# The seventh key chunk of an attention head as one full-width matmul, late queries and keys loaded in whole rows, and a new written order of the work

## The chip, the cores and the metric

The kernel runs on one core of one Trainium2 chip. The metric is the device time of one execution in microseconds (us). An effect of about 1% (4 us of 401) is what a measurement of this kernel can tell from no change.

## The reference

Attention with a squared ReLU in place of the softmax, for 8 batches of 12 heads, 448 positions and 64 values per head, and behind it a gated feed-forward block on the 3584 tokens:

```python
# q, k, v: (8, 12, 448, 64)
scores = scale * np.matmul(q, k.transpose(0, 1, 3, 2))     # scale = 1/8
attn = np.maximum(scores, 0.0) ** 2 / S                     # S = 448
attn_out = np.matmul(attn, v)
x = attn_out.transpose(0, 2, 1, 3).reshape(B * S, H * D)    # (3584, 768)
g, val = x @ w_gate, x @ w_val                              # (768, 1536) each
out = (gelu(g) * val) @ w_out                               # (1536, 768)
```

Inputs and the output are float32; the kernel computes in bfloat16 with float32 sums.

## The kernel before, in words

**The array in quarters.** Heads are 64 wide, so every matmul of the steady work uses one 64x64 quarter of TensorE: two row groups (where the operands' partitions lie) by two column groups (where the output's partitions lie). Four quarters work side by side. A helper `mm` (L365 in the profile) records all of these matmuls, so they share one line and are told apart by their tiles.

**Attention.** The 448 positions of a head are cut into 7 key chunks of 64. Two chunks `w` and `w + 4` (`w` = 0, 1, 2) make one score unit of two heads: four matmuls of 448 columns, one in each quarter, into two banks of PSUM (tile `sp`). ScalarE applies the ReLU to the whole unit (tile `rl`, L714), VectorE squares (tile `attnT`, L728), mostly two units at once. The chunk with index 3 (`VC - 1`) has no partner. Before, its units take four heads at once, and the queries are halved: each head's matmul of 64 keys and 448 queries is run as two of 224 queries, one in each column group, so that a unit has eight matmuls of 224 columns. A head pair's values (`add_values`) are sums over the chunks: row group 0 takes chunks 0, 1, 2, row group 1 takes chunks 4, 5, 6, and chunk 3 is split between the two row groups, each with 224 columns. The result is copied as `xT` (L792).

**Feed-forward.** Some blocks of 128 features are computed plainly: gate (`xT,wg`) and value (`xT,wv`) matmuls of 448 columns in `add_gate_value`. For the others (`NPB`: 0, 1, 2, 3, 4, 4, 6, 6 units for batches 0 to 7) seven products of half size take the place of eight (`add_pair`, 224 columns each); these need sums of weight blocks (`add_pair_sums`, VectorE, L870, tiles `ws`) and of token blocks (`ts`). The output product works in the same manner on two chunks of tokens (`add_product`, 384 columns, tiles `s`, `wt`, `osb`), 14 groups lettered a to n.

**Loads.** All loads of inputs go through the POOL queue, in one written order: queries, keys and values of batches 0 and 1 with the weights between them, then the "late" batches 2 to 7. Batches 0 and 1 get their transposed queries and keys from TensorE (`add_transposes`, L646, four heads at a time for batch 1); the late ones from VectorE's copy `qkr` (L475) and two DMA transposes on the SP queue. Before, late queries and keys come in two pieces per tensor: the first four chunks of four heads, then the last three.

**What sets the order.** The table `START` orders batch 0's attention. `LINE` lists the feed-forward units (a digit: a plain gate or value unit of that batch; `3A4`: a seven-product unit; `f2`: an output product). Scores and values of batches 1 to 7 are placed between them by a formula (`starts`, `LEAD`, `SHIFT`). `run_plan`, a planner with costs in us, walks this list: among the next 40 units (`AHEAD`) it takes the first whose inputs it expects to be there, and it also decides where the row-group-1 half of each unit, the copies, the stores and the DMA transposes go. So the list is a preference, and the program's order is the planner's. Banks of PSUM: four for the feed-forward and two pairs for scores; once the scores of batch 1 are done (`WIDE`) one pair is handed to the feed-forward.

Of the kernel before, what the change touches and what calls it, by code (L numbers as in the profile page):

```python
# [11 lines left out]
LINE = """  # L12
0 0 0 0 0 0 0 0 0 0 0 0 0 0 0 0 0 0 0 0 0 0 0 0 1 1A1 1 2 1A6 2 2 1 1A7 1A2 1A5 2 a1 2 a2 2A1 1A4 1
1 1 1A3 1 2 1 2A2 a6 1 2A7 a7 2 1 a5 1 1 2A6 2 2 1 1 1 1 a3 1 1 a4 1 1 b1 b7 c1 b2 b6 2A4 2 c6 b4 b5
c7 c5 2B1 2B6 c4 2B2 c3 b3 2A5 2 c2 2B7 2B4 2B5 2A3 2 3A1 2 3A2 2 2B3 2 2 3A6 3A7 d7 d1 3B1 d2 4C1
3B2 3 3C1 3B7 3 d6 3 e1 d4 3C7 3 3C6 3 3B6 e7 3B4 e6 3A4 3A5 3 3 3 3C2 3 3B5 3 3 d5 3C4 3A3 3C5 d3
4A1 4C2 3B3 3C3 e5 3 4A7 f1 f2 f6 e4 f7 4C7 4 e2 4C6 4A2 e3 g7 4B1 f5 4B6 4 4A6 4B2 g1 4B7 4 g2 4A5
4C5 4A4 4B4 4B5 f4 4D7 4D1 4C4 4 5B1 5 4D6 4D5 4A3 4 g6 4 g5 4C3 4B3 f3 4 5 5B2 4D2 4D4 g3 4D3 5C1
g4 5B6 5B7 5C2 5B5 5A1 4 5A6 5 5C7 5A7 5A2 5 5B4 5D1 h1 5A4 5D6 5D2 h6 5C6 h7 5 5D7 5D5 5A5 6A1 5B3
5 5C5 5C4 5A3 5C3 5D4 6B1 5 5D3 5 6A2 6B2 h4 i1 i2 6B7 6A6 i7 h5 6A7 h2 6D1 6F7 6D7 h3 j1 6D6 6C1  # L20
6D2 i6 j7 6E1 j6 6C7 6C2 6E7 i5 i4 6C6 6B6 6A5 6A4 6E6 6A3 6F1 6B4 6B5 6C5 6D5 6D4 6F6 i3 6B3 6F5
6C4 j5 6D3 6E2 6F2 6E5 6F4 6C3 6F3 6E4 6E3 7E7 j2 7E1 7B1 k1 k7 7E2 7A1 7B2 7B7 k2 7B6 7E6 j4 7C1 k6
7A2 l7 7C7 7C6 7A7 7B4 7C2 l1 7B5 7B3 k5 7A6 7F1 j3 7D1 7E5 7F7 7F2 7A5 k4 7F6 7E4 l6 7D7 7C4 7D2
7F4 7D6 7D5 7D4 7D3 l2 7F5 7A4 7C5 7C3 7E3 7A3 l5 l4 7F3 m1 n1 m7 k3 l3 m2 m6 n6 m5 n7 n4 m3 n5 n2
m4 n3
# [7 lines left out]


SHIFT = "-183 -79.5 40.75 1.75 -343.75 -112 43.75 -179.5 27.25 -513.5 -447.25 0.25"
# [60 lines left out]
class Unit:  # L96


    def __init__(self, at, los, his, box=None, closer=None, prev=None):
        self.at, self.los, self.his, self.box, self.closer, self.prev = at, los, his, box, closer, prev  # L100
        self.begun = False
        self.short = False
# [3 lines left out]
BANK = 0.3  # L106


def run_plan(queues, pools, units, banks, arrivals, together, fill, blocks, span):
# [48 lines left out]
    def next_unit(short):  # L158
        best = None
        now = max(free["PE0"], floor)  # L160
        for u in units[:AHEAD]:
# [16 lines left out]
            if u.box is not None:  # L178
                k, end = None, None
                for n, c in banks.items():  # L180
                    x = 0.0 if c is None else c.end
                    if x is not None and (end is None or x < end):
                        k, end = n, x
                if k is None:
                    continue
                t = max(t, end + BANK)
            if short and t > now:
                continue
            t = max(t, now)
            if best is None or t < best[0]:  # L190
                best = (t, u, k)
                if t <= now:
                    break
# [5 lines left out]
    while left:  # L199
# [33 lines left out]
        if isinstance(op, tuple):  # L233
            _, u, k = op
            u.begun = True
            units.remove(u)
            if k is not None:
                u.box["k"] = k
                banks[k] = u.closer()
            queues["PE0"][at["PE0"]:at["PE0"]] = u.los  # L240
# [36 lines left out]
def kernel(  # L277
# [42 lines left out]
    SINGLE = "3"  # L320
    RING_M, RING_G = 5, 4
# [17 lines left out]
    loaded = tc.tile_pool(name="lpool", bufs=2), tc.tile_pool(name="hpool", bufs=RING_H)  # L339
# [75 lines left out]
    def load_qk(b, i, h0, h1, deps=()):  # L415

        src = (q, k)[i]
        m, r0 = divmod(h0, 4)

        def emit(c0, c1):  # L420
            if (b, m) not in qk16:
                qk16[b, m] = hpool.tile([128, 4, SC * D], bf16, name="qk16", tag="qk16")
            cols = slice(c0 * D, c1 * D)
            return nc.gpsimd.dma_start(  # L424
                qk16[b, m][HALF[i], r0:r0 + h1 - h0, cols],
                src[b, h0:h1].rearrange("h (p c) d -> p h (c d)", c=SC)[:, :, cols])
# [39 lines left out]
    def add_dma_transposes(b, m, deps=()):  # L466
# [23 lines left out]
        copy = Op("DVE", 0.62, emit_copy, [wait, *(regrouped[n - 2] if n > 1 else ())], lag=0.15, prio=1)  # L490
# [43 lines left out]
    def next_scores(at):  # L534

        n = len(units)
        if at > WIDE and n % SB == 0 or wide:
# [48 lines left out]
    def then(at, step, los, his, box=None, closer=None):  # L586

        if not isinstance(at, list) and at > FIXED:
# [3 lines left out]
            later.append(Unit(at, los, his, box, closer))  # L592
# [84 lines left out]
    def add_scores(at, b, u):  # L677
# [9 lines left out]
        def emit(j, pr):  # L687
# [73 lines left out]
    def add_values(at, b, pr):  # L761
        box = {}

        order = ([0, 3, 1, 2] if pr % 2 else [0, 1, 2, 3], [3, 0, 1, 2])
# [3 lines left out]
        def emit(i, w):  # L768
            if 0 not in box:
                box[0] = new_bank(box["k"], x_op[b, pr])  # L770
            if (i, w) == (1, VC - 1) or last and (i, w) == (0, 1):
                wait_lower(box)
            for j in range(2):
                o = box[0][HALF[j], 0:S]
                a = att[b, pr, w][HALF[i], j, :]
                if w < VC - 1:
                    ins = mm(o, v16[b, pr // 2][HALF[i], 2 * (pr % 2) + j, w + i, :], a, i, j,
                       i == 0 and w == 0, i == 1 - last and w == VC - 2)
                else:
                    ins = mm(o.rearrange("d (c p) -> d c p", c=SC)[:, :, i * P // 2:(i + 1) * P // 2],  # L780
                       v16[b, pr // 2][HALF[i], 2 * (pr % 2) + j, (1 - i) * (VC - 1), :],
                       a[:, (pr % 2) * S // 2:(pr % 2 + 1) * S // 2].rearrange(
                           "k (c p) -> k c p", c=SC), i, j, False, False)
# [11 lines left out]
        ops = [[Op(f"PE{i}", 0.189 if w < VC - 1 else 0.095, lambda i=i, w=w: emit(i, w),  # L795
# [18 lines left out]
        if last:  # L814
            ops[1][0].after = ops[0][1]
            for o, p in zip(ops[1], ops[1][1:]):
                p.after = o
            ops[0][2].deps.append(ops[1][3])
            for i in range(2):
                lower.append((at - 0.6, ops[0][i]))  # L820
                lower.append((at, ops[0][i + 2]))
            for hi in ops[1]:
                pairs.append(("with", ops[0][1], hi))
# [285 lines left out]
    def add_sums(gr):  # L1109
# [20 lines left out]
        def add(n, x, y, op, into=None, after=(), cuts=(0, KH)):  # L1130
# [14 lines left out]
            for f0, f1 in zip(cuts, cuts[1:]):  # L1145
# [8 lines left out]
                for b in {b for t, _ in tiles for b, _ in chunks[t]}:  # L1154
                    if st["made_by"](b, 0) is u_op[b, 0]:
# [4 lines left out]
    def add_product(at, gr, name, final):  # L1160
# [100 lines left out]
        for b in {b for tile in chunks for b, _ in tile}:  # L1261
            if st["made_by"](b, 0) is u_op[b, 0]:
                reads_u.setdefault(b, []).append(ops[1][-1])
        then(at, RS, *ops, box if name in opens else None, lambda: st["read", stages_last[stage]])
# [38 lines left out]

    work = []
    flow = [[("g", b, fc, g) for fc in range(2 * NPB[b], FC) for g in range(2)] for b in range(B)]
    line = []
    for x in LINE.split():
        if len(x) == 1:
            line.append(flow[int(x)].pop(0))
        elif len(x) == 3:  # L1310
            line.append(("7", int(x[0]), "ABCDEFGHIJKL".index(x[1]), x[2]))
        else:
            line.append(("p", "abcdefghijklmn".index(x[0]), x[1]))
    assert not any(flow)
# [182 lines left out]
```

## Time and profile before

| | |
|---|---|
| median of 3 runs | 401.29 us (399.08 to 402.02) |
| span of the profiled execution | 394.9 us; the page gives this execution by its span alone, and the median lies 6.39 us above it |
| instructions in the span | 22904, of them 10570 matmuls and 10573 weight loads |
| TensorE busy | 386.3 us, 98% |
| VectorE, ScalarE busy | 309.6 us (78%), 258.7 us (66%) |
| granted TensorE clock | 0.998 |
| read and written in HBM | 48.76 MB, 11.01 MB |

The span is the time from the first to the last instruction that the profiler recorded. Busy time of TensorE is that of modelled, overlapping matmuls: it says that the engine was not empty, not how full it was. A row of a group gives the count, the busy time, the mean duration of one in ns, and the idle time of its engine just ahead of it with what ended it. POOL's rows are the issue of loads; when the data lands is seen from who waits for it.

### The profile page before, as it was taken

To read this page: it belongs to the slowest core of one execution; us is meant where nothing else is said; L and a number is where in the kernel's file an instruction comes from. 1 tells how busy PE (TensorE), PEld (TensorE's weight loads), DVE (VectorE), ACT (ScalarE), POOL (GpSimd) and SP (SyncE) were. 2 spreads that over 40 slices of the span, in tenths; PEclk is the share of its full clock that TensorE was granted. 3 is DMA by queue.
4 is the path that set the end of the run, shared out by engine and by line. 5 is a ranking of instruction groups with operands and counts; after the bars stand their busy time and mean duration, and the time that the engine had idled before them with its cause. 6 is when DMAs were issued, how large, how long until landed. Compare 5 with 4: busy or idle time off the path is not lost.

```text
span 394.9 us, 22904 instructions
## 1 busy us (share of the span) xinstructions
PE 386.3 (98%) x10570; PEld 358.4 (91%) x10573; DVE 309.6 (78%) x522; ACT 258.7 (66%) x401; POOL 97.2 (25%) x156
## 2 busy tenths in 40 slices
PE   7999999999999999999999999999999999999995
PEld 3458889999999999999999999989999999999994
DVE  3885779968797499999797779758988999866772
ACT  5866872357677767787786478765787886535541
POOL 7656523322233323232332123310211000000000
PEclk9999999999999999999999999999999999999999
DMA  8999999988999969887999598880763501121134
GB/s 110 186 199 199 197 209 185 112 103 83 161 148 175 152 85 143 93 132 121 113 148 108 124 122 111 139 83 11 103 105 56 125 6 43 45 45 45 43 85 120
DMA packets 85567, 45.12 MB, mean 114 GB/s; under 512 B 46048, under 2 KB 82400, under 8 KB 85472
## 3 DMA queue, kind: packets, MB, share of 16 engines
q0 software_dynamic: 46944, 24.39, 49.9%
q1 hardware_dynamic: 37888, 18.49, 26.4%
q8 instruction: 82, 1.34, 1.4%
q10 hardware_dynamic: 640, 0.79, 0.6%
q14 instruction: 13, 0.11, 0.1%
HBM read 48.76 MB, written 11.01 MB: 151 GB/s over the span
## 4 chain that ended last, share of the span: by engine, by line
PE 93%; DVE 2%; DMA 2%; POOL 1%; issue 1%; ACT 0%; ACTq 0%; POOLq 0%
PE ff L365 85%; PE sp L365 7%; DMA qk<-in_k_dram 2%; DVE attnT L728 1%; PE sp L646 1%; POOL qk L424 1%; DVE xT L792 0%; PE ff L646 0%; ACTq L1241 0%; ACT osb L1225 0%; ACT rl L714 0%; PE ff L567 0%; DVE osb L1223 0%; DVE qkT L650 0%; POOL ident masks.py:199 0%
## 5 line engine op out<-in xcount | busy, mean ns | idle before, releaser
L714 ACT ACTIVATE rl<-sp 128x896 bf16<-128x896 f32 x168 | 152.1, 919 | 50.4 <-PE sp L365 45.1
L365 PE MATMUL ff<-xT,wg 64*64 64x224 bf16 (+1 forms) x2304 | 183.7, 299 | 0.6 <-issue 0.6
L365 PEld LDWEIGHTS <-wv 64*64 64x64 bf16 x2304 | 127.7, 107 | 4.4
L365 PEld LDWEIGHTS <-wg 64*64 64x64 bf16 x2304 | 123.3, 107 | 5.0 <-issue 0.5
L365 PE MATMUL ff<-xT,wv 64*64 64x448 bf16 x1056 | 120.8, 349 | 0.0
L728 DVE TENSOR_TENSOR attnT<-rl 128x1792 bf16<-128x1792 bf16 (+1 forms) x98 | 92.2, 952 | 6.6 <-ACT rl L714 6.2
L365 PEld LDWEIGHTS <-ws 64*64 64x64 bf16 x1872 | 92.3, 107 | 1.4 <-issue 1.0
L365 PEld LDWEIGHTS <-s 64*64 64x64 bf16 x1344 | 81.6, 107 | 1.8
L365 PE MATMUL ff<-attnT,v 64*64 64x448 bf16 (+1 forms) x768 | 79.7, 326 | 0.7 <-DVE attnT L728 0.6
L365 PE MATMUL ff<-ts,wv 64*64 64x224 bf16 x1248 | 78.7, 256 | 0.0
L365 PE MATMUL ff<-ts,ws 64*64 64x224 bf16 x1248 | 77.6, 256 | 0.0
L365 PE MATMUL sp<-qkT 64*64 64x448 bf16 (+1 forms) x768 | 74.6, 328 | 0.7 <-issue 0.3
L365 PE MATMUL ff<-wo,s 64*64 64x384 bf16 x672 | 63.4, 323 | 0.0
L966 DVE TENSOR_TENSOR part<-ff,part 128x448 f32<-128x448 f32 x78 | 47.5, 622 | 20.1 <-PE ff L365 16.4
L365 PEld LDWEIGHTS <-uT 64*64 64x64 bf16 x1008 | 62.5, 107 | 0.7
L365 PE MATMUL ff<-wt,s 64*64 64x384 bf16 x672 | 61.4, 322 | 0.0
L365 PE MATMUL ff<-wo,uT 64*64 64x384 bf16 x672 | 60.7, 322 | 0.0
L962 ACT COPY part<-ff 128x448 f32<-128x448 f32 x78 | 41.3, 534 | 12.4 <-PE ff L365 11.2
L443 POOL DMA_DIRECT2D v<-in_v_dram x48 | 29.6, 620 | 80.3 <-ACT rl L714 44.3
L365 PEld LDWEIGHTS <-v 64*64 64x64 bf16 x768 | 44.7, 107 | 4.1 <-issue 1.7
L424 POOL DMA_DIRECT2D qk<-in_q_dram x43 | 27.6, 642 | 80.0 <-ACT rl L714 59.5
L1049 DVE TENSOR_TENSOR uT<-gel,ff 128x448 bf16<-128x448 bf16 x44 | 27.3, 620 | 22.4 <-PE ff L365 11.0
(51 smaller groups left out, 423.9 us busy)
## 6 DMA issues: line engine op xcount, KB each, us to landing
out_dram<-osb SPq DMA_DIRECT2D x48, 192.0 KB, 3.3
v<-in_v_dram POOLq DMA_DIRECT2D x48, 128.0 KB, 4.1
wg<-in_moe_w_gate_dram POOLq DMA_DIRECT2D x6, 384.0 KB, 10.4
wv<-in_moe_w_val_dram POOLq DMA_DIRECT2D x6, 384.0 KB, 11.0
wo<-in_moe_w_out_dram POOLq DMA_DIRECT2D x4, 576.0 KB, 14.9
qk<-in_q_dram POOLq DMA_DIRECT2D x18, 128.0 KB, 3.5
qk<-in_k_dram POOLq DMA_DIRECT2D x18, 128.0 KB, 4.3
qk<-in_q_dram POOLq DMA_DIRECT2D x18, 96.0 KB, 3.8
```

Of the source, the lines that this page charges most:

```text
L365: ins = nc.tensor.matmul(o, lhsT, rhs, start=start, stop=stop, skip_group_check=onto, tile_position=(P * row, P * col))
L424: return nc.gpsimd.dma_start(qk16[b, m][HALF[i], r0:r0 + h1 - h0, cols], src[b, h0:h1].rearrange("h (p c) d -> p h (c d)", c=SC)[:, :, cols])
L443: return nc.gpsimd.dma_start(v16[b, m][HALF[i], h0 % 4:h0 % 4 + h1 - h0, :, :], v[b, h0:h1].rearrange("h (p c) d -> p h c d", c=SC)[:, :, ...
L646: blocks.add(nc.tensor.transpose(t[HALF[j], c, :], src[:, 2 * r + j, c, :], ident[:, :], tile_position=(0, P * j)))
L714: relu.ins = nc.scalar.activation(duo["rl"][:, u % 2, :, :], box[0][:, :, 0:S], AF.Relu).ins
L728: nc.vector.tensor_tensor(a[:, part], duo["rl"][:, part], duo["rl"][:, part], op=ALU.mult)
L962: rd.ins = nc.scalar.copy(st["t", name][:, :], box[0][:, 0:S]).ins
L966: rd.ins = nc.vector.tensor_tensor(t[:, :], box[0][:, 0:S], t[:, :], op=ALU.add).ins
L1049: u_op[b, fc].ins = nc.vector.tensor_tensor(uT[b][:, fc, :], gel.pop((b, fc))[:, :], box[0][:, 0:S], op=ALU.mult).ins
```

## The change

1. **The seventh chunk whole.** In a score unit of chunk 3, each head now has one matmul of 448 queries; the two head pairs of the unit lie in the two column groups. So the unit has four matmuls of 448 columns in place of eight of 224. In `add_values` chunk 3 then belongs to one row group alone: to row group 0 for even head pairs (four steps there, three in row group 1), to row group 1 for odd ones (three and four). This is 96 matmuls fewer in the scores and 96 fewer in the values, each with its weight load: 384 instructions.
2. **Late queries and keys in whole rows.** A load takes two heads and all seven chunks (`64x2x448`) in place of four heads and four or three chunks.
3. **The order.** `LINE` now names every unit of batches 1 to 7: `s` a score unit, `v` a value unit, `t` a transpose unit of batch 1, `w0` to `w5` the weight sums of a block; the formula and `SHIFT` are gone. `START` and `run_plan`'s rules stay, but for an option (`more`, `full`, `COVER`) that no caller uses. `WIDE` now counts score units (44) and means the same place.

On TensorE, around the third group of transposes of batch 1 (`qk16`: heads 8 to 11), with the values of batch 1's first pair (`attnT,v16`) and gate and value units of batch 0 (`xT,wg`, `xT,wv`), before:

```order
L365 MATMUL ff_1020<-attnT_935,v16_534 64x448
...
L365 MATMUL ff_975<-xT_393,wg2_131 64x448
...
L365 MATMUL ff_1020<-attnT_935,v16_534 64x7x32
...
L365 MATMUL ff_1039<-xT_393,wv2_137 64x448
...
L646 LDWEIGHTS qk16_689
L646 MATMUL sp_1051<-ident_121,qk16_689 64x128
```

The same place of the change:

```order
L385 MATMUL ff_930<-attnT_837,v16_516 64x448
...
L385 MATMUL ff_890<-xT_385,wg1_130 64x448
...
L385 MATMUL ff_958<-xT_385,wv1_136 64x448
...
L665 LDWEIGHTS qk16_662
L665 MATMUL sp_971<-ident_121,qk16_662 64x128
```

The transposes, which stood behind the first units of weight block 2 (`wg2`, `wv2`), now stand ahead of them, among those of block 1. Ahead of them stood 398 matmuls of 448 columns and 58 of 224; now 382 of 448. The fourth step of a value unit, 224 columns as 7x32, is a whole one of 448.

On VectorE in the same stretch (squares `attnT`, transposed keys `qkT`, gated features `uT`, attention output `xT`), before:

```order
L728 TENSOR_TENSOR attnT_787<-rl_719 128x1792
L650 COPY qkT_811<-sp_756 128x7x128
L1049 TENSOR_TENSOR uT_824<-gel_804,ff_634 128x448
...
L1049 TENSOR_TENSOR uT_824<-gel_846,ff_745 128x448
L728 TENSOR_TENSOR attnT_935<-rl_817 128x1792
L1049 TENSOR_TENSOR uT_824<-gel_928,ff_856 128x448
L728 TENSOR_TENSOR attnT_985<-rl_882 128x1792
```

and in the change:

```order
L741 TENSOR_TENSOR attnT_837<-rl_778 128x1792
L1055 TENSOR_TENSOR uT_812<-gel_831,ff_717 128x448
L876 TENSOR_TENSOR ws10_888<-wv0_135 128x768
L741 TENSOR_TENSOR attnT_906<-rl_848 128x1792
L876 TENSOR_TENSOR ws20_935<-ws10_888,wg0_129 128x768
L1055 TENSOR_TENSOR uT_812<-gel_922,ff_855 128x448
L876 TENSOR_TENSOR ws40_969<-wg0_129,ws20_935 128x768
L741 TENSOR_TENSOR attnT_989<-rl_900 128x1792
```

The sums of weight block 0, which stood behind the last square of batch 1's attention, now stand inside it; two of the four of block 1 (`ws11`, `ws21`) follow there too.

On the POOL queue, the first late loads behind the last weights, before:

```order
L412 DMA wo3_144<-in_moe_w_out_dram 128x3x768
L424 DMA qk16_962<-in_q_dram 64x4x256
L424 DMA qk16_962<-in_q_dram 64x4x192
L424 DMA qk16_962<-in_k_dram 64x4x256
L424 DMA qk16_962<-in_k_dram 64x4x192
L424 DMA qk16_1091<-in_q_dram 64x4x256
```

and in the change:

```order
L432 DMA wo3_144<-in_moe_w_out_dram 128x3x768
L443 DMA qk16_928<-in_q_dram 64x2x448 x2
L443 DMA qk16_928<-in_k_dram 64x2x448 x2
L443 DMA qk16_1022<-in_q_dram 64x2x448 x2
L443 DMA qk16_1022<-in_k_dram 64x2x448 x2
L462 DMA v16_1161<-in_v_dram 64x4x256 x2
```

Four loads stay four, with the same bytes in all; only their cut differs, and the place in the queue is the same.

```diff
 LINE = """
-0 0 0 0 0 0 0 0 0 0 0 0 0 0 0 0 0 0 0 0 0 0 0 0 1 1A1 1 2 1A6 2 2 1 1A7 1A2 1A5 2 a1 2 a2 2A1 1A4 1
...
+0 s s t s 0 0 0 0 s v s s s s s t 0 0 v s s s s 0 v 0 0 w0 a7 s v 0 0 0 0 0 0 0 s s s s 0 s s s s v
...
-SHIFT = "-183 -79.5 40.75 1.75 -343.75 -112 43.75 -179.5 27.25 -513.5 -447.25 0.25"
...
     def load_qk(b, i, h0, h1, deps=()):
...
-        for c0, c1, rate in (((0, SC, 400e3 if b else (300e3, 226e3, 420e3)[m]),) if b < EARLY
-                             else ((0, VC, 390e3), (VC, SC, 350e3))):
-            op = load(4 * (h1 - h0) * P * (c1 - c0) * D, lambda c0=c0, c1=c1: emit(c0, c1), deps, rate=rate)
+        rate = 400e3 if b else (300e3, 226e3, 420e3)[m]
+        for g0, g1 in ((h0, h1),) if b < EARLY else ((h0, h0 + 2), (h0 + 2, h1)):
+            op = load(4 * (g1 - g0) * P * SC * D, lambda g0=g0, g1=g1: emit(g0, g1), deps, rate=rate)
...
     def add_scores(at, b, u):
...
-            for i in range(2):
-                if tail:
-                    n0 = (pr % 2) * S // 2
-                    qs = t[:, :, i * P // 2:(i + 1) * P // 2]
-                    mm(sp[HALF[i], j, n0:n0 + S // 2].rearrange("k (c p) -> k c p", c=SC),
-                       t[:, VC - 1, HALF[1]], qs, j, i, True, True)
-                else:
-                    mm(sp[HALF[i], j, 0:S].rearrange("k (c p) -> k c p", c=SC),
-                       t[:, cl + i * VC, HALF[1]], t[:, :, HALF[0]], j, i, True, True)
+            for i in (pr % 2,) if tail else range(2):
+                mm(sp[HALF[i], j, 0:S].rearrange("k (c p) -> k c p", c=SC),
+                   t[:, VC - 1 if tail else cl + i * VC, HALF[1]], t[:, :, HALF[0]], j, i, True, True)
...
     def add_values(at, b, pr):
...
-        order = ([0, 3, 1, 2] if pr % 2 else [0, 1, 2, 3], [3, 0, 1, 2])
+        order = ([0, 1, 2], [3, 0, 1, 2]) if pr % 2 else ([0, 1, 2, 3], [0, 1, 2])
...
-        ops = [[Op(f"PE{i}", 0.189 if w < VC - 1 else 0.095, lambda i=i, w=w: emit(i, w),
+        ops = [[Op(f"PE{i}", 0.189, lambda i=i, w=w: emit(i, w),
...
-    for i in reversed(range(max(NPB))):
-        behind = [n for n, w in enumerate(work) if w[2] is add_gate_value and w[3][0] == first_use(i) - 1][-1]
-        work.insert(behind + 1, (0.0, 5, lambda at, i: add_pair_sums(i), (i,)))
+    for n, x in enumerate(LINE.split()):
+        at = 1.0 + n
+        if x[0] == "w":
+            work.append((0.0, lambda at, i: add_pair_sums(i), (int(x[1]),)))
+        elif x == "s":
+            work.append((at, add_scores, flow_s.pop(0)))
+        elif x == "v":
+            work.append((at, add_values, flow_v.pop(0)))
+        elif x == "t":
+            work.append((at, add_transposes, flow_t.pop(0)))
+        elif len(x) == 1:
+            work.append((at, add_gate_value, flow[int(x)].pop(0)[1:]))
...
+    WIDE = 44
```

More of the change, by code (lines that the diff above doesn't have):

```diff
@@ L18 @@
[L18 to L22, printed above, removed]
@@ L106, with run_plan @@
 BANK = 0.3
-def run_plan(queues, pools, units, banks, arrivals, together, fill, blocks, span):
+COVER = 0.06
+def run_plan(queues, pools, units, banks, full, arrivals, together, fill, blocks, span):
     free = {e: 0.0 for e in (*queues, *pools)}
@@ L186, in next_unit @@
                 t = max(t, end + BANK)
+            k2 = None
+            if u.more is not None:
+                for n, c in banks.items():
+                    x = 0.0 if c is None else c.end
+                    if n != k and n in full and x is not None and (k2 is None or x < end):
+                        k2, end = n, x
+                if k2 is None:
+                    continue
+                t = max(t, end + BANK)
             if short and t > now:
@@ L239, in run_plan @@
                 banks[k] = u.closer()
+                full[k] = u.full
+            if k2 is not None:
+                u.more[0]["k"] = k2
+                banks[k2] = u.more[1]()
+                if not full[k2]:
+                    u.more[0]["cover"] = True
+                    u.los[0].cost += COVER
+                full[k2] = True
             queues["PE0"][at["PE0"]:at["PE0"]] = u.los
@@ L320 @@
     SINGLE = "3"
+    RING_L = 2
     RING_M, RING_G = 5, 4
@@ L584, in both, with then @@
             pairs.append(("with", lo, hi))
-    def then(at, step, los, his, box=None, closer=None):
+    def then(at, step, los, his, box=None, closer=None, more=None, full=True):
         if not isinstance(at, list) and at > FIXED:
@@ L1379 @@
+    WIDE = 44
+    for at, fn, args in work:
         fn(at, *args)
```

166 lines of the change are left out of this document (63 added, 103 removed).

## The prediction

> **What bounds the kernel now.** First the page's totals, then the slices of 10 us (columns: the stretch and its length; for each engine busy us and instructions; the granted clock; the DMA engines' share and GB/s).
>
> ```profile
> span 394.9 us, 22904 instructions
> PE 386.3 (98%) x10570; PEld 358.4 (91%) x10573; DVE 309.6 (78%) x522; ACT 258.7 (66%) x401; POOL 97.2 (25%) x156
> ...
> 0.00:10.00 10.00, 7.98 (x78) 3.79 (x79) 3.09 (x8) 5.50 (x8) 7.88 (x18) 1.00 0.82 111
> 20.00:30.00 10.00, 9.14 (x161) 5.35 (x158) 8.75 (x16) 5.85 (x8) 5.40 (x8) 1.00 1.37 199
> 30.00:40.00 10.00, 10.00 (x220) 8.31 (x215) 5.21 (x8) 6.86 (x10) 6.60 (x9) 1.00 1.41 198
> 40.00:50.00 10.00, 10.00 (x230) 8.65 (x224) 7.52 (x10) 7.92 (x11) 4.88 (x7) 1.00 1.45 197
> 50.00:60.00 10.00, 10.00 (x219) 8.24 (x214) 7.18 (x11) 7.40 (x10) 2.69 (x5) 1.00 1.20 210
> 310.00:320.00 10.00, 10.00 (x343) 9.91 (x337) 9.36 (x16) 9.15 (x16) 0.00 (x0) 1.00 0.31 83
> 330.00:340.00 10.00, 10.00 (x364) 9.94 (x358) 9.45 (x19) 4.98 (x10) 0.00 (x0) 1.00 0.18 40
> ```
>
> TensorE (PE) is never empty from 30 us on, at full clock. But matmuls overlap, so "10.00" alone doesn't say that the array is full. For that, all matmuls by form in one slice, 330 to 340 us (count | busy us, mean ns of one | idle before):
>
> ```profile
> L365 PE MATMUL ff<-xT,wg 64*64 64x224 bf16 x108 | 5.5, 256 | 0.0
> L365 PE MATMUL ff<-ts,wv 64*64 64x224 bf16 x78 | 5.1, 256 | 0.0
> L365 PE MATMUL ff<-wo,uT 64*64 64x384 bf16 x44 | 4.3, 322 | 0.0
> L365 PE MATMUL ff<-attnT,v 64*64 64x448 bf16 x24 | 3.1, 349 | 0.0
> L365 PE MATMUL ff<-ts,ws 64*64 64x224 bf16 x48 | 3.1, 256 | 0.0
> L365 PE MATMUL ff<-xT,ws 64*64 64x224 bf16 x37 | 2.6, 256 | 0.0
> L365 PE MATMUL ff<-wo,s 64*64 64x384 bf16 x17 | 1.8, 322 | 0.0
> L365 PE MATMUL ff<-attnT,v 64*64 64x224 bf16 x8 | 1.1, 256 | 0.0
> ```
>
> A matmul of 448 columns lasts 349 ns, one of 224 lasts 256: 224 columns more cost 93 ns, so a column streams in 0.415 ns and the rest is pipeline that overlaps. The eight groups hold 279 matmuls of 224, 61 of 384 and 24 of 448 columns, 96,672 columns; in four quarters at 0.415 ns that is 10.03 us, in a slice of 10.00 us with some of its matmuls hanging over the edges. The array is full there: **what bounds the kernel is the number of columns**.
>
> What is left is stalls. The waits of PE from 47 us to the end are one line; the chain of waits shows where it is. I also read the chain at the third group of batch 1's transposes (start us, length us, what):
>
> ```profile
> PE ff L365 <- issue: 0.6, 1, 0.6
> ...
> 42.66 0.90 PE sp L646 x28
> ...
> 264.60 0.87 PE ff L365 x37
> 265.47 0.65 issue
> ...
> 327.91 60.72 PE ff L365 x1677
> 388.66 0.57 DVE osb L1223
> ```
>
> From 47 us on PE waits once, 0.6 us, for nothing that the profile shows ("issue", at 265.47). The last 6.2 us (394.9 - 388.7) are the last matmuls, additions, copies and stores. So there is little to win outside the first 47 us, and anything that makes PE wait is paid in full.
>
> **The change part by part.**
>
> *The seventh chunk.* 384 matmuls of 224 columns become 192 of 448. Columns: 384 x 224 = 192 x 448, so the streaming stays. What may go is a fixed cost per matmul. The slice above bounds it: 364 matmuls, of which some eight hang over (0.25 us); 10.00 us and those 0.25 us leave at most 0.22 us over the 10.03 us of streaming, 0.6 ns a matmul. 192 times that is 0.1 us. I take -0.1; the bounds are -0.3 and 0.
>
> The Trainium skill's page "TensorEngine Tiling (Array Packing)", section "Instruction Overhead", says that each matmul has about 60 cycles of overhead. By that the 192 would be worth more; the rival below works it out, and the slice above, 364 matmuls that leave no room for it, speaks against it.
>
> *The row groups.* A value unit now has four steps in one row group and three in the other instead of 3.5 and 3.5. A half step is 224 columns, 93 ns. If none of the 48 units could fill the other row group with its neighbours' matmuls, 48 x 0.093 = 4.5 us would be added; if all do, nothing. In the order's rows a value step of row group 0 stands beside a gate or value unit's step of row group 1, and even and odd pairs lean to opposite sides. I take 0, near the slice in which the same mixture leaves no gap; the range keeps 0 and +4.5.
>
> *The fillers.* The order has two matmuls of 512 columns on `warm` fewer, in the start. They only fill waits: 0; at most 2 x 512 x 0.415 ns = -0.4 us.
>
> *The third transposes of batch 1.* They stand behind 382 matmuls of 448 columns instead of 398 of 448 and 58 of 224: 45 x 448 columns less, in four quarters 2.1 us earlier, and up to 0.4 us more with the fillers. They need the keys that this load brings:
>
> ```profile
> 30.39 0.61 POOL L424 DMA_DIRECT2D qk<-in_q_dram  x1 [0.63 <-PE sp L365]
> 31.63 0.61 POOL L424 DMA_DIRECT2D qk<-in_k_dram  x1 [0.64 <-DMA qk<-in_k_dram]
> ...
> 40.24 0.82 POOL L404 DMA_DIRECT2D wv<-in_moe_w_val_dram  x1 [0.29 <-DMA qk<-in_k_dram]
> ```
>
> The weight load at 40.24 waited 0.29 us for a load of keys, so these land at about 39.95. PE came at 42.66; now it would come at 42.66 - 2.1 - 0.4 = 40.16 at the earliest. **The margin shrinks from 2.7 to 0.2 us.** TensorE takes its matmuls in order here, so whatever is missing stops the units behind it as well. Value 0; if the start runs half a us faster than before, up to +0.5.
>
> *The weight sums moved forward.* Six sums of `ws` now stand among batch 1's squares:
>
> ```profile
> L870 DVE TENSOR_TENSOR ws<-ws,wg 128x768 bf16<-128x768 bf16 x6 | 3.3, 552 | 0.0
> ```
>
> 6 x 0.552 = 3.3 us. What hides them: VectorE (DVE) is busy 5.21 + 7.52 + 7.18 = 19.9 us between 30 and 60, and 10.1 us are free. Behind each sum queue a square, on which a value unit depends, and copies of `qkT`, on which the next scores depend. Without that cover all 3.3 us are paid. I take 0, because three times the room is there; the range keeps +3.3.
>
> *Late loads in whole rows.* 72 issues stay 72, the bytes stay:
>
> ```profile
> qk<-in_q_dram POOLq DMA_DIRECT2D x18, 128.0 KB, 3.5
> qk<-in_k_dram POOLq DMA_DIRECT2D x18, 128.0 KB, 4.3
> qk<-in_q_dram POOLq DMA_DIRECT2D x18, 96.0 KB, 3.8
> qk<-in_k_dram POOLq DMA_DIRECT2D x18, 96.0 KB, 4.0
> ```
>
> A piece of 96 KB took as long to land as one of 128, and the pieces to come are 112 KB; I expect 3.5 to 4 us. Since PE waits for no load after 47 us, this is worth 0 either way.
>
> *The rest of the order.* The same number of instructions runs on VectorE (522) and ScalarE. No ten microseconds of matmul work hold more than seven score units, before or now (counted in the order); seven ReLUs of 0.92 us are 6.4 us of ScalarE:
>
> ```profile
> L714 ACT ACTIVATE rl<-sp 128x896 bf16<-128x896 f32 x168 | 152.1, 919 | 50.4 <-PE sp L365 45.1
> ```
>
> The slice 310 to 320 carried 9.15 us of ScalarE and 9.36 of VectorE with PE full. I take 0. The stall of 0.65 us at 265 may vanish or come elsewhere: 0, bounds -0.65 and +0.65 for each one more. The last products, additions and stores stand in the same pattern as before: 0.
>
> Sum: -0.1 us. Span 394.9 - 0.1 = 394.8; with the 6.39 us by which the median of the runs lies above this span, **401.2 us**. The single runs before spread from 399.08 to 402.02, so 1 to 2 us either way come from that alone.
>
> **The rivals.**
>
> *Slower by the row groups.* The place: the 48 value units; the price 93 ns each; it decides as soon as the planner's neighbours don't fill the lighter row group in nearly all of them. For it: the units were balanced before. Against: the planner starts a unit's second half beside the next unit's first. All of it: 401.2 + 4.5 = 405.7 us.
>
> *Slower in the start.* Sums not hidden and keys late: 401.2 + 3.3 + 0.5 = 405.0. For it: 20 to 30 us is VectorE's at 8.75. Against: the sums come after it, where a third is free.
>
> *Slower by more issue stalls.* Each costs 0.65 us; seven more give 401.2 + 4.55 = 405.8. For it: the profile has one already, and the instructions sit elsewhere in the stream now. Against: one in 394.9 us. The Trainium skill, page "Runtime: NRT & Kernel Launch", section "Instruction fetch mechanics", says that instructions are fetched in blocks of 256 and the cost is mostly hidden. That the stall was such a fetch no row here shows.
>
> *Faster by a fixed cost per matmul.* If a matmul cost 25 ns (60 columns' time) besides its columns, and the smaller ones hid it badly, 192 x 25 = 4.8 us would go in a row, 1.2 us in four quarters: 396.4 to 400.0. With 0.65 from the stall: 395.8. Against: the slice, 0.6 ns.
>
> *The change doesn't do what it says.* The queries' order or a planner's choice could keep two matmuls: the order shows 20760 rows on TensorE for 21148, so it does; time 401.3.
>
> **How the numbers follow.** Forecast, the same pace within 2 us, 399 to 403: 0.61. Row groups 0.10 (405.7, slower). Start 0.10 (half beyond 1%). Issue stalls 0.05 (slower). Fixed cost 0.12 (0.10 beyond 1%, with what else the order may win). No effect 0.02. An effect of 1%, 4 us, is about what a measurement of this kernel can tell from no change: faster ends at 397.3, slower starts at 405.3. So faster 0.10; slower 0.10 + 0.05 + 0.05 = 0.20; same 0.70. The range 397.5 to 405.7 takes in the bounds of the row groups and the start, and leaves out the lower end of the fixed cost.
>
> **What would show it.** The page after has some 22,520 instructions and about 10,380 matmuls, none of 224 columns on `sp`. Right: the chain is PE at about 98% with no wait over 1 us after 47 us, the third transposes begin at 40 to 41 us without an idle stretch ahead, the slices from 60 to 380 hold PE at 10.00, and the last matmul ends within 1 us of 388.35 + 2.38 = 390.73:
>
> ```profile
> 388.35 2.38 PE L365 MATMUL ff<-wo,s 64*64 64x384 bf16 x36
> ```
>
> Row groups: more time everywhere at equal counts, no wait named. Start: waits of PE for `attnT` or `qkT` before 60 us. The forecast is wrong if the chain names another engine for more than a few us, or if a stretch of full PE has another rate per column.

## The result and the profile after

The changed kernel takes **398.07 us** (median of 15 runs, 396.69 to 400.07), the kernel before took 400.66 us beside it (15 runs, 397.94 to 404.52). The ratio is **0.9945, 95% interval 0.9921 to 0.9969**: 0.55% or 2.2 us faster. The ratio is of the means of the fast runs, without the one slow run of before (404.52 us); the medians differ by 2.6 us. Where several kernels are compared below, each ratio is to the kernel before on the same chip at the same time.

The page of the changed kernel: totals, the packets of instructions, and the shares of the chain.

```profile
span 395.1 us, 22511 instructions
...
PE 387.6 (98%) x10379; PEld 355.5 (90%) x10379; DVE 309.2 (78%) x522; ACT 259.3 (66%) x401; POOL 95.3 (24%) x156
...
q8 instruction: 81, 1.33, 1.4%
...
PE 93%; DMA 2%; DVE 2%; ACT 1%; issue 0%; ACTq 0%
```

The slices of 10 us that answer to those shown of before, and three in which TensorE has a hole:

```profile
20.00:30.00 10.00, 9.39 (x151) 5.34 (x151) 8.85 (x16) 5.81 (x7) 5.76 (x9) 1.00 1.37 200
30.00:40.00 10.00, 10.00 (x210) 7.95 (x206) 6.70 (x11) 8.09 (x12) 6.44 (x10) 1.00 1.41 199
40.00:50.00 10.00, 10.00 (x213) 8.02 (x208) 8.57 (x14) 7.07 (x10) 4.86 (x7) 1.00 1.45 196
50.00:60.00 10.00, 10.00 (x220) 8.83 (x216) 8.75 (x14) 7.08 (x10) 2.37 (x4) 1.00 1.21 209
...
80.00:90.00 10.00, 9.55 (x250) 9.15 (x251) 5.07 (x7) 7.77 (x12) 3.00 (x5) 1.00 0.68 95
...
140.00:150.00 10.00, 9.91 (x259) 8.63 (x253) 8.95 (x14) 7.08 (x11) 3.00 (x5) 1.00 0.85 111
...
350.00:360.00 10.00, 9.81 (x342) 9.27 (x336) 5.49 (x10) 5.52 (x11) 0.00 (x0) 1.00 0.32 82
```

The only wait of TensorE that the profile names from 47 us on (us in total, times, the longest):

```profile
PE sp L385 <- DMA qkT<-qkr: 0.4, 1, 0.4
```

The load in POOL's timeline that waits for the last keys of batch 1:

```profile
39.79 0.82 POOL L424 DMA_DIRECT2D wv<-in_moe_w_val_dram  x1 [0.31 <-DMA qk<-in_k_dram]
```

TensorE's timeline: the first half of the third transposes of batch 1, which need these keys, and the last matmuls:

```profile
40.60 0.58 PE L665 MATMUL sp<-ident,qk 128*64 128x128 bf16 x14
...
388.48 2.38 PE L385 MATMUL ff<-wo,s 64*64 64x384 bf16 x36
```

The two pages are almost the same: the span is 395.1 us for 394.9, and the last matmul ends at 390.86 us for 390.73. **The pair of profiles does not hold the 2.2 us.** Something in the other executions does. For those there are the spans of every timed run:

```
                        runs   time, mean   span, lowest   span, mean   time - span, mean
before, beside b_full7   34      401.4         396.5          398.9           2.5
after                    15      398.3         394.5          396.1           2.2
```

So the profiled execution of before, 394.9 us, was faster than every one of 34 later executions of the same kernel; a usual one is some 4 us longer (mean spans of 398.9 us here, 397.6 and 399.3 in the two later batches of experiments). The execution that I read lacked something that a usual one has.

### The profile page after: what moved, and what is told of

It is laid out like the page before. It is cut to its first block, busy times and chain, and to the rows that moved or that the text cites. A ratio compares the mean times of both kernels' runs of the same rounds, so it can differ in the third digit from the quotient of the medians.

```text
span 395.1 us, 22511 instructions
## 1 busy us (share of the span) xinstructions
PE 387.6 (98%) x10379; PEld 355.5 (90%) x10379; DVE 309.2 (78%) x522; ACT 259.3 (66%) x401; POOL 95.3 (24%) x156
## 4 chain that ended last, share of the span: by engine, by line
PE 93%; DMA 2%; DVE 2%; ACT 1%; issue 0%; ACTq 0%
PE ff L385 82%; PE sp L385 8%; DMA qkT<-qkr 2%; DVE attnT L741 1%; PE ff L1399 1%; ACT rl L727 1%; PE sp L665 1%; PE ff L586 1%; DVE xT L798 0%; PE ff L665 0%; ACTq L1247 0%; ACT osb L1231 0%; PE ff L628 0%; DVE osb L1229 0%; DVE qkT L669 0%
## 5 line engine op out<-in xcount | busy, mean ns | idle before, releaser
L385 PE MATMUL ff<-xT,wg 64*64 64x224 bf16 (+1 forms) x2304 | 177.6, 299 | 0.0
L385 PEld LDWEIGHTS <-wg 64*64 64x64 bf16 x2304 | 120.3, 107 | 4.7
L385 PEld LDWEIGHTS <-wv 64*64 64x64 bf16 x2304 | 120.6, 107 | 4.2 <-issue 0.5
L385 PE MATMUL ff<-xT,wv 64*64 64x448 bf16 x1056 | 113.4, 349 | 0.1
L385 PE MATMUL sp<-qkT 64*64 64x448 bf16 x672 | 81.2, 352 | 0.9 <-DMA qkT<-qkr 0.4
L385 PEld LDWEIGHTS <-s 64*64 64x64 bf16 x1344 | 78.0, 107 | 2.9 <-issue 0.2
L385 PE MATMUL ff<-attnT,v 64*64 64x448 bf16 x672 | 78.0, 349 | 0.7 <-DVE attnT L741 0.5
L385 PEld LDWEIGHTS <-uT 64*64 64x64 bf16 x1008 | 58.1, 107 | 2.1 <-issue 0.3
L1231 ACT COPY osb<-ff 128x384 f32<-128x384 f32 x56 | 26.7, 480 | 30.7 <-PE ff L385 30.3
L385 PEld LDWEIGHTS <-v 64*64 64x64 bf16 x672 | 39.9, 107 | 4.4 <-issue 1.9
```

The lines of the kernel that those rows point to most:

```text
L385: ins = nc.tensor.matmul(o, lhsT, rhs, start=start, stop=stop, skip_group_check=onto, tile_position=(P * row, P * col))
L1231: ins = nc.scalar.copy(o, box[0][:, 0:OGS])
```

## The experiments

### The parts apart

Four kernels with one or two of the three parts. "Old list" is the old `LINE` with the formula and `SHIFT`; the planner runs again where the instructions on TensorE differ.

`b_full7`: the old list, the seventh chunk whole.

```diff
     def add_scores(at, b, u):
...
-            for i in range(2):
-                if tail:
...
+            for i in (pr % 2,) if tail else range(2):
+                mm(sp[HALF[i], j, 0:S].rearrange("k (c p) -> k c p", c=SC),
+                   t[:, VC - 1 if tail else cl + i * VC, HALF[1]], t[:, :, HALF[0]], j, i, True, True)
...
     def add_values(at, b, pr):
...
+            if w == VC - 1 and i != pr % 2:
+                return
```

> The kernel before with the old list and formula; only the seventh chunk is run whole (384 instructions fewer). Theory ORDER (the 2.2 us come from the new written order): 1.000 of before, within 0.3%. Theory COUNT (a fixed cost per matmul, 2.2 us / 192 = 11 ns each): 0.9945, that is 398.5 us beside 400.7. Theory LOADS (whole rows): 1.000.

Measured: 402.92 us, ratio 1.0049 (1.0019 to 1.0079). None of the three theories had this: slower.

`b_whole`: the old list, the late loads in whole rows.

```diff
-            cols = slice(c0 * D, c1 * D)
...
+            g0, g1 = (h0, h1) if b < EARLY else (h0, h0 + 2) if c0 == 0 else (h0 + 2, h1)
...
```

> The kernel before with only the cut of the late queries and keys changed (two heads and seven chunks a load); every other engine's order is that of before, word for word. ORDER: 1.000. COUNT: 1.000. LOADS: 0.9945.

Measured: 400.75 us, ratio 0.9981 (0.9951 to 1.0011).

`b_both`: both of these edits, the old list.

> The kernel before with the seventh chunk whole and the late loads in whole rows, and the old list: the change without its new order. ORDER: 1.000 within 0.3%. COUNT: 0.9945. LOADS: 0.9945.

Measured: 403.64 us, ratio 1.0039 (1.0006 to 1.0073).

`a_pieces`: the change with the late loads in the old pieces.

```diff
+            cols = slice(0, SC * D) if b < EARLY else slice(0, VC * D) if g0 == h0 else slice(VC * D, SC * D)
...
-                qk16[b, m][HALF[i], g0 - 4 * m:g1 - 4 * m, :],
...
+                qk16[b, m][HALF[i], h0 - 4 * m:h1 - 4 * m, cols],
...
```

> The changed kernel with the late queries and keys in the old pieces (four chunks of four heads, then three); every other engine's order is that of the change. ORDER: 0.9945. COUNT: 0.9945. LOADS: 1.000.

Measured: 398.14 us, ratio 0.9925 (0.9891 to 0.9958).

The cut of the loads is worth nothing, with either list, so LOADS falls. The whole seventh chunk alone makes the kernel slower by 0.5%, so COUNT falls. ORDER is nearest, but it had 1.000 for `b_full7` and `b_both`, and both are slower. From `b_both` (1.0039) to the change (0.9945) only the order differs: **the new order is worth about 0.9%**, and it pays for the 0.4% that the rest costs. But why? In `b_full7` the waits of TensorE from 47 us on say it:

```profile
PE ff L365 <- issue: 3.1, 6, 1.6
PE sp L365 <- DMA qkT<-qkr: 0.5, 1, 0.5
PE sp L365 <- issue: 0.2, 1, 0.2
```

It waits longest for nothing that the profile names, the "issue" of which the profile of before had one. And its array is as fast as before where nothing waits: between 200 and 250 us the columns of all matmuls at 0.415 ns, in four quarters, make up 48.8 us of the 50, in before 48.9, in the change 48.9.

### Where TensorE waits for nothing

The longest such holes of three profiles, each with the matmul ahead of it (before, `b_full7`, `a_pieces`; start us, length us, what, and the idle time ahead):

```profile
265.21 0.26 PE L365 MATMUL ff<-xT,wg 64*64 64x224 bf16 x1
266.12 0.25 PE L365 MATMUL ff<-xT,wg 64*64 64x224 bf16 x1 [0.65 <-issue]
```

```profile
81.98 0.26 PE L365 MATMUL ff<-xT,ws 64*64 64x224 bf16 x2
83.80 0.38 PE L365 MATMUL ff<-xT,wv 64*64 64x448 bf16 x2 [1.56 <-issue]
```

```profile
141.34 0.38 PE L385 MATMUL ff<-attnT,v 64*64 64x448 bf16 x2
143.68 0.38 PE L385 MATMUL ff<-xT,wv 64*64 64x448 bf16 x2 [1.96 <-issue]
```

A row gives the idle time behind the end of the matmuls ahead. From here on a hole is the time from one instruction's start to the next one's, so it is longer, and a hole that the running matmuls cover shows as no wait at all. From the start of one row to the next are 0.91, 1.82 and 2.34 us. Now I count TensorE's instructions in the trace from the start of the program: weight loads, matmuls and the few waits of its sequencer. The hole of before stands behind the 13,246th, that of `b_full7` behind the 3,006th, that of `a_pieces` behind the 5,822nd. These are 190 + 51 x 256, 190 + 11 x 256 and 190 + 22 x 256. The others too: from 47 us on, in all 14 profiles of this case, each hole of more than 0.38 us that isn't a wait for transposed keys (`DMA qkT<-qkr`) stands at **190 plus a multiple of 256** (193 in the change's profile, which has three records more). In the change's profile the queue of instruction packets holds 81 packets of 16 KB, and the 20,792 instructions counted are 81 times 256 and a few more. So TensorE's program comes in blocks of 256 instructions, and at the end of a block it waits until the next has landed.

The trace has the start and length of each of these packets. Each block has one, which mostly starts about 1 us behind the block's first instruction. For the 94 holes of over 0.25 us at the ends of blocks, behind 64 us in the 14 profiles, the next block's first instruction starts 1.43 us (standard deviation 0.12) behind the end of the packet. So a block costs little as long as it lasts until some 1.35 us behind its packet's landing: of the 1008 blocks behind 64 us, 145 last less than that, and 93 of the 94 holes are among them.

A block of 128 matmuls with their weight loads lasts as long as its columns: with 448 columns each 128 x 448 x 0.415 / 4 = 5.9 us, with 224 only 3.0 us. The packets of before land 1.9 us (median) behind the block's start, so 3.3 us are needed, and more where the packet is late. Blocks full of 224-column matmuls are at the limit.

The table is worked out of the traces' records, one profiled execution a row, from 47 us to the last products: "short" are blocks that last less than 3.8 us without the hole at their end, and stalls are the holes at the ends of blocks less 0.05 us each.

```
                       blocks  short   stalls us: all, behind short, behind other   packet lands, us behind block start
old order  before          75     22      1.2   0.9   0.3                                1.89
           b_whole         75     22      3.6   2.3   1.4                                2.12
           b_shift256      76     22      3.7   1.8   1.9                                2.33
new order  after           75     14      1.0   0.3   0.6                                1.88
           a_pieces        75     15      3.1   0.8   2.3                                2.00
           a_nomark        75     15      0.8   0.0   0.8                                1.84
           a_shift256      75     15      0.5   0.0   0.5                                1.98
           a_loads         75     15      1.9   1.3   0.7                                2.06
old list, whole chunk
           b_full7         74     17      6.2   2.4   3.7                                2.13
           b_both          74     15      5.5   2.3   3.3                                2.05
moved      a_shift32       75     15      3.9   1.6   2.2                                2.02
           a_shift224      75     15      5.5   2.7   2.8                                2.18
           a_shift128      74     19      7.3   5.1   2.2                                2.30
           b_shift128      75     18      9.1   3.1   6.0                                2.38
```

The span less these stalls is 394.8 us in the mean over the 14 profiles, with a standard deviation of 1.0, while the spans themselves go from 394.5 to 403.6. The stalls at the ends of blocks are the larger part of what differs.

That is a count in traces. The next runs move the ends of the blocks against the work, and keep the order of the work.

### The ends of the blocks moved

The 16 warm-up matmuls at the very start are cut into more pieces with the same columns, and the planner doesn't hear of it. Every later instruction stands further on in TensorE's stream, in the same order on all engines, word for word.

```diff
 def emit_warm_up():
...
-                blocks.add(nc.tensor.matmul(t[HALF[j], :], warm[:, HALF[j]], warm[:, :],
-                                            start=True, stop=True, tile_position=(0, P * j)))
+                cut = [512 * n // 5 for n in range(5 + 1)]
+                for n, (c0, c1) in enumerate(zip(cut, cut[1:])):
+                    ins = nc.tensor.matmul(t[HALF[j], c0:c1], warm[:, HALF[j]], warm[:, c0:c1],
+                                           start=True, stop=True, tile_position=(0, P * j))
+                    if n == 0:
+                        blocks.add(ins)
```

Here each is cut into 5 pieces, 64 matmuls more, that is 128 places with their weight loads; 9 pieces give 256 places, 2 give 32 and 8 give 224.

> The changed kernel with its order word for word, but its 16 warm-up matmuls of 512 columns in the start are cut into 80 of 102 or 103 columns: the same columns, 64 matmuls with their weight loads more, so every later instruction stands 128 places further on in TensorE's stream. Theory FETCH (TensorE stalls where a block of 256 of its instructions ends before the next one is fetched; the new order wins by what happens to stand at those places): the places move by half a block against the work; stalls again at every 256th instruction, at other work; 398 to 402 us, likely slower than the change by 1 to 4 us. Theory ORDER-ELSE (the new order wins by something else, such as waits for data): 398.1 within 0.3%, ratio 0.9945.

Measured: 403.67 us, ratio **1.0096** (1.0060 to 1.0133). That is above the 402 us that FETCH had given at most.

> As the run with 64 matmuls more, but 128 more (16 of 512 columns cut into 144 of 56 or 57): 256 places, a whole block, so the ends of the blocks fall on the same work as in the change. FETCH: as the change, 398.1 within 0.3%. ORDER-ELSE: the same. If it is slower as well, the extra matmuls in the start cost it, and the run with 128 places tells nothing.

Measured: 398.99 us, ratio **0.9975** (0.9946 to 1.0004).

> The kernel before with its order word for word and 128 places more, made as in the changed kernel. FETCH: 399 to 404 us, either way of 401.3, with the stalls at other work (none of 0.9 us at 265 us). ORDER-ELSE: 1.000 within 0.3%.

Measured: 407.84 us, ratio **1.0191** (1.0134 to 1.0247), from six runs where the others have twelve. This too is above FETCH's range, which ended at 404 us.

> The kernel before, order word for word, 256 places further on, a whole block: the ends of the blocks fall on the same work as before. FETCH: 1.000 of before within 0.4%, where 128 places gave 1.019. If the extra matmuls in the start cost it: 1.004 or more.

Measured: 401.26 us, ratio **0.9981** (0.9956 to 1.0006).

Half a block costs the new order 1.5% and the old one 1.9%. A whole block, with twice as many matmuls added, costs the new order 0.3%, with an interval that overlaps the change's, and the old one nothing. The waits of TensorE from 47 us on, of `a_shift128`, `a_shift256` and `b_shift128`:

```profile
PE ff L385 <- issue: 3.3, 6, 1.1
PE sp L385 <- issue: 0.3, 1, 0.3
```

```profile
PE sp L385 <- DMA qkT<-qkr: 0.3, 1, 0.3
```

```profile
PE ff L365 <- issue: 4.2, 8, 1.1
PE sp L365 <- issue: 0.2, 1, 0.2
PE ff L365 <- PE ff L365: 0.2, 1, 0.2
```

The longest holes now stand at other work and still at the count of 256: `a_shift128` behind the 12,222nd (190 + 47 x 256), `b_shift128` behind the 11,710th (190 + 45 x 256). The hole of `b_shift128`, at an output product (`wo,uT`) and token sums (`ts,wv`) where before had none:

```profile
241.69 0.26 PE L365 MATMUL ff<-ts,wv 64*64 64x224 bf16 x1
243.11 0.28 PE L365 MATMUL ff<-ts,wv 64*64 64x224 bf16 x2 [1.12 <-issue]
```

So ORDER-ELSE falls, and FETCH is shown as far as it says that TensorE stalls at the ends of blocks: an order that isn't changed by a single row loses 6 to 8 us when its blocks end half a block away. FETCH had the loss too small.

What decides how much is lost isn't shown. The number of short blocks isn't enough: `b_shift128` has 18 of them, before 22, and yet it has the longest stalls. And the move changes one thing more. The kernel's planner itself counts blocks of 256 (class `Blocks`, in both kernels): it ties the late DMA transposes to a matmul a little ahead of a block's end, and holds a later store that would fall around a block's end until the end is past. The cut warm-up matmuls, of which the planner doesn't hear, move the real ends away from these places. By the traces, 17 of the change's 18 stores of the SP queue behind 302 us are issued in the first 2 us of a block; of those of `a_shift128` it is 1 of 17, of `a_shift224` 13 of 16. Whether the half block costs time by the matmuls at the ends or by transfers that no longer stand where they were planned, no run separates.

Two smaller moves tell how finely that place counts.

> The changed kernel, order word for word, 32 places further on in TensorE's stream (16 warm-up matmuls of 512 columns cut into 32 of 256). By the profile of the change the ends of the blocks then fall so that its shortest blocks are as long as before (3.48 us the shortest, for 3.44). LENGTH: 398.1 within 0.4%. If the places of the DMA transposes and loads against the ends of blocks decide as well: between the change and the run with 128 places, 398 to 401.

Measured: 399.79 us, ratio 0.9943 (0.9918 to 0.9967): as the change, though the one profiled execution has 3.9 us of stalls for the change's 1.0.

> The same with 224 places more, that is 32 places back from a whole block (16 warm-up matmuls cut into 128 of 64 columns). LENGTH: 0 to 1 us slower than the change, its shortest block 3.35 us. Otherwise 398 to 401, as with 32 places.

Measured: 403.55 us, ratio 1.0041 (1.0010 to 1.0072): 1% slower than the change.

32 places on are free, 32 places back cost 1%. LENGTH alone gave the second 0 to 1 us, but it lost 4: the number of short blocks is the same 15 as with 32 places, and the stalls are 2.7 us behind those and 2.8 behind longer ones. So how long the blocks are doesn't explain it all; by the table, how late the packets land counts as well.

### What makes the packets late

The packets that land late mostly do it where DMA transposes run. In the 14 profiles, behind 64 us: with a transpose in flight between the block's start and the packet's landing, 66 of 617 packets land more than 3.2 us behind the block's start (the latest 5.9 us); without one, 8 of 391. `a_nomark` lets go of the pacing of the transposes:

```diff
 def emit_transpose(i, c0, c1):
-            if tr_op[b, m][i].mark is not None:
-                tc.add_manual_dep(ins.ins, tr_op[b, m][i].mark.ins.name, SYNC, reason="pace")
```

> The changed kernel with its order word for word, but the DMA transposes of the late queries and keys no longer wait for a matmul that stands a little ahead of the end of an instruction block; they go as soon as their data and their turn are there. FETCH with the transposes as what delays the fetches: more fetches late, 399 to 402 us. FETCH without the transposes, or ORDER-ELSE: 398.1 within 0.3%.

Measured: 397.34 us, ratio 0.9944 (0.9915 to 0.9972): no change, and not the 399 to 402 us of FETCH with the transposes. Only 18 of the 36 transposes lose their wait for TensorE by it; the others keep one, and the stores stay held. So for these 18 the pacing is worth nothing where the blocks end as planned; whether the transposes themselves make packets late, the run doesn't decide.

`a_loads` adds traffic where there is little, behind 300 us:

```diff
+    spare = [const.tile([128, 256], bf16, name=f"spare{n}") for n in range(2)]
...
+    for n in range(36):
+        nc.gpsimd.dma_start(spare[n % 2][:, :], moe_w_gate[0:128, 0:256])
```

> The changed kernel with its order word for word and, behind the last load of values, 36 more loads of 128 KB each into a spare tile, two at a time; nothing waits for them. They fall behind 300 us, where the kernel loads nothing, and where a block of 256 instructions lasts 3.4 to 4.5 us. Theory TRAFFIC (loads in flight make the instruction fetches late): the fetches behind 300 us land later than the 2.0 us behind a block's start of before, and the stalls there add up to 2 to 5 us: 400 to 403 us. Theory LENGTH (only how long a block lasts decides): no more stalls, 398.1 within 0.4%.

Measured: 399.90 us, ratio 0.9953 (0.9924 to 0.9982). Two slices of the change and the same two of `a_loads` (the last columns: granted clock, DMA share, GB/s):

```profile
320.00:330.00 10.00, 10.00 (x332) 9.91 (x326) 9.52 (x16) 8.23 (x15) 0.00 (x0) 1.00 0.02 5
330.00:340.00 10.00, 10.00 (x348) 9.94 (x340) 9.06 (x18) 5.93 (x11) 0.00 (x0) 1.00 0.19 43
```

```profile
320.00:330.00 10.00, 10.00 (x334) 9.89 (x327) 9.52 (x16) 8.23 (x15) 3.18 (x6) 1.00 0.32 38
330.00:340.00 10.00, 10.00 (x348) 9.91 (x342) 9.06 (x18) 5.93 (x12) 2.86 (x6) 1.00 0.51 81
```

The loads are there (0.51 for 0.19 of the DMA engines), and the packets from 302 to 370 us land 2.17 us behind the blocks' starts in the mean, for 2.07 in the change and 1.9 to 2.1 in the other unmoved or whole-block profiles of the new order. The stalls there are 0.7 us for 0.6, not the 2 to 5 us of TRAFFIC, and the ratio is the change's within its interval. So at these loads TRAFFIC falls; a delay of 0.1 us can't be told from chance with one execution each.

Nor do I know why the packets of the kernels moved by 128 and 224 places land later, 2.2 to 2.4 us in the median for 1.8 to 2.1 in the new order's other profiles; from 302 to 370 us, where no transposes are left, it is 2.3 us in the mean for 2.1 in the change. The stores that no longer stand where they were planned are a candidate that no run tests. They can't be all: `b_shift256`, whose blocks end as planned, has 2.3 us in the median as well. That stays open.

## Why the prediction was right or wrong

The forecast was 401.2 us and no change of more than 1%; the time is 398.07 us, within the range, and the change is 0.55%. So the outcome was right and the sum, -0.1 us, too small: the measured gain is 2.2 us. That the time lies in the range is in part luck: it is 0.6 us above the lower end, and the mechanism that moved it was in the sum with 0.

**Right.** *The bound.* Outside the stalls both kernels keep nearly the pace that the columns set. *The seventh chunk.* 192 matmuls fewer buy no pace: 48.9 us of columns in the 50 us from 200 to 250, before and after. *The row groups* (4.5 us at most) show no cost of that size: the change's span less the stalls at block ends is 395.1 - 1.0 = 394.1 us, before's 394.9 - 1.2 = 393.7. *The third transposes.* I had PE there at 40.16 us at the earliest and the keys at 39.95; it was 40.60 and, read in the same way (39.79 less the wait of 0.31), 39.48, without a wait. *The sums of `ws`.* VectorE has 6.70 + 8.57 + 8.75 = 24.0 us between 30 and 60, 4.1 more than before, and TensorE has no wait there that the profile names. *The loads.* 112 KB land in 3.3 and 3.8 us:

```profile
qk<-in_q_dram POOLq DMA_DIRECT2D x38, 112.0 KB, 3.3
qk<-in_k_dram POOLq DMA_DIRECT2D x38, 112.0 KB, 3.8
```

and `b_whole` shows that it is worth nothing. *A fixed cost per matmul* falls: `b_full7` has the 384 instructions fewer and is slower, and its span less the stalls, 402.6 - 6.2 = 396.4 us, isn't shorter than before's 393.7.

One sign that I had named for being right didn't come: the slices from 60 to 380 us don't all hold TensorE at 10.00; three have 9.55, 9.91 and 9.81.

**The step that was mis-sized** is the term of "the stall of 0.65 us at 265": "0, bounds -0.65 and +0.65 for each one more". It was the only trace of the mechanism that decides this change. By one execution I took it as a single event; in fact each of some 80 block ends can stall, by 0 to 2.3 us, and the stalls of the old order are 1.2, 3.6 and 3.7 us in three profiles, those of the new one 1.0, 3.1, 0.8, 0.5 and 1.9. The means, 2.8 and 1.5, differ by 1.4 of the 2.2 us. Nearly all of that lies behind short blocks (1.7 and 0.5 us), of which the new order has 14 or 15 for 22. With three and five executions this is a reading, not a measurement: the mean spans of these same profiles differ by only 1.1 us, and with `a_shift32` (3.9 us, as fast as the change) the new order's mean would be 1.9. Nor does every pair of kernels show the order's gain: moved by half a block the new order is 0.9% faster than the old one (1.0096 for 1.0191), but moved by a whole block they have 0.9975 and 0.9981, on two chips, with intervals of 0.3% either way. Measured is that the order gains where nothing is moved, and that moving the block ends moves the time by more than the whole gain; that the gain comes by fewer short blocks isn't shown.

**The second wrong step** was to add "the 6.39 us by which the median of the runs lies above this span" as if it were one constant. Only 2 to 2.5 us of it lie around the span in the mean of later runs. The other 4 are what the profiled execution happened not to have. Part of them are most likely these stalls: the two other profiles with the old order, `b_whole` and `b_shift256`, are 3.2 and 4.0 us longer, and 2.4 and 2.5 us of that are stalls at block ends. A span so far under the median was the hint that "there is little to win outside the first 47 us" was read from a lucky run.

**The rivals.** "Slower by more issue stalls" named the mechanism that the runs show, with the wrong sign for the whole change: it came true for the half of the change that `b_full7` is (stalls of 6.2 us, 1.0049) and for the moved kernels. The Trainium skill, page "Runtime: NRT & Kernel Launch", section "Instruction fetch mechanics", says that TensorE's instructions come in blocks of 256 and that the cost of crossing into the next is mostly hidden. The count of 256 is what the holes show; "mostly hidden" holds for 59 to 74 of some 75 blocks in these profiles (those without a hole over 0.2 us), and the rest is worth up to 9 us.

What I had not foreseen is a wait of 0.4 us at 80.5 us, for the second transpose of the first late queries and keys. TensorE comes to these scores at 79.5 us where it came at 81.2, and the transpose lands at 80.45 us for 81.19.

## What to carry to other kernels

When TensorE is full, look for holes that the profile puts down to "issue" and count the instructions up to them: if they come at a fixed stride, as here at 256, the engine is likely waiting for its own instructions, and the place of the block ends in the order is a parameter like any other. Many short matmuls in a row make a block that can be over before the next has landed; mixing them with long ones is what the table suggests, and no run tests it alone. And compare the profiled execution's span with the spans of the timed runs before reading from it what there is to win: a lucky execution hides just what varies.

## What the runs showed of the hardware

- 64 more matmuls in the first microseconds, at the same columns and with the order of all else untouched, cost 1.5% and 1.9% of the whole kernel; 128 more cost nothing or 0.3%.
- Where TensorE stalled at the end of a block of 256 of its instructions, the next block began 1.43 us behind the landing of its packet. The packets landed 1.8 to 2.4 us behind the start of the running block in the median, and up to 5.9 us at worst.
- Loads of 128 KB, two at a time, delayed these packets by no more than 0.1 us (2.17 us in the mean for 2.07) and cost no time.
